# Cached attention decode on one core: each load of keys and values issued as two halves, by SyncE and by ScalarE

## The chip, the cores and the metric

The kernel runs on one core of a Trainium2 chip. The metric is the device time of one execution in microseconds (us), the median of the runs shown; less is better. The profile is of one further execution, and its times are in us from its own start.

## What is computed

One token of a small transformer block: layer norm, attention of 32 heads over a cache of 32768 keys and values of 128 numbers each, a residual, then layer norm and an MLP with the mish activation. All arrays are bfloat16. Cut to what matters:

```python
def _A_ref(x, k_cache, v_cache, wq, wo):          # x [1,1,512], caches [1,32,32768,128]
    q = (x @ wq).reshape(1, 1, 32, 128).transpose(0, 2, 1, 3)
    scores = jnp.einsum("bhqd,bhkd->bhqk", q, k_cache) * (128 ** -0.5)
    p = softmax(scores)
    o = jnp.einsum("bhqk,bhkd->bhqd", p, v_cache)
    return o.transpose(0, 2, 1, 3).reshape(1, 1, 4096) @ wo

h = x + _A_ref(layernorm(x), ...)
h2 = h + mish_mlp(layernorm(h), w1, b1, w2)       # 512 -> 1376 -> 512
```

The two caches hold 32 x 2 x 8.39 MB = 537 MB; all the weights together are 11 MB. Every byte of them is read once.

## The kernel before

**Tiles.** A head's keys are one load of 8.39 MB: partition p takes the 256 consecutive keys 256p to 256p+255, a run of 64 KB, as 256 tiles of 128 x 128 (r-th tile: the r-th key of every partition). Values are laid out the same way. SBUF has a buffer `ring` of six slots of 32 KB a partition: slots 0 and 1 are the home of the keys (`khome`), 2 and 3 that of the values, 4 holds wq (later w1 and w2), and in slot 5 lies `kcopy`, room for the keys' last 112 tiles. So there is one home for keys and one for values, and each serves all heads in turn.

**A head** (function `one`, a loop over heads on TensorE and VectorE). TensorE transposes the keys in 32 groups of 8 tiles (L510), VectorE copies each group from PSUM to `ering` (L513), TensorE multiplies it with the query (L481). `soft_max`, `soft_a`, `soft_b` find the maximum over all scores and, with the next head's query (L539, L543), take a few microseconds; ScalarE's exp (L556) writes the weights `pbuf`; `pv` (L524) multiplies them with the values, 256 small matmuls; `oev` (L531) writes the head's output. To free the keys' home early, ScalarE copies their last 112 tiles to `kcopy` as soon as they have landed (L571, `kc`). Groups 0 to 17 are read from the home, 18 to 31 from the copy.

**Who frees what** (`freed_by`). The next head's keys may be loaded when the 18th group has been transposed (`kfree`) and the copy has been made (`kc`). The next head's values may be loaded when the last matmul of `pv` has read the old ones (`free`). wo follows when the keys' home is free at the end, w1 and w2 when the last query has been made (`qm32`).

**The order of loads.** SyncE issues all loads in one list (`order`): wq, then per head keys and values, then wo, w1, w2. It waits for what frees the target, then issues (L364, in `start`). Heads 0, 30 and 31 are `PARTED`: their keys come in two loads, the first 144 tiles to the home and the last 112 straight into `kcopy`, so ScalarE makes no copy there; head 31's first part is cut once more, and its values come in two halves, the second with a semaphore of its own (`s_half`). ScalarE issues two small loads at the start, x (L407) and b1 (L408), ahead of its table load (L410).

**Waits for data.** Slot 0's semaphore `ready[0]` counts the keys' loads, 16 for each; TensorE waits for 16(h+1) ahead of group 0 and ScalarE ahead of its copy. `ready[2]` counts the values' the same way. `ready[1]` and `s_half` are raised by GpSimd for the heads in which they aren't used.

**Loops.** `rounds` writes a head's work as a hardware loop for the engines in `LOOPED`, the waits as multiples of the loop counter; `apart` leaves some heads outside of it. ScalarE has head 0 ahead of its loop and heads 30 and 31 behind it. SyncE and GpSimd have straight-line programs.

Of the kernel before, what the change touches and what calls it, by code (L numbers as in the profile page):

```python
# [11 lines left out]
AXX = mybir.AxisListType.X  # L12

PE, ACT, DVE, POOL, SP = "pe", "act", "dve", "pool", "sp"
LOOPED = {PE: mybir.EngineType.PE, DVE: mybir.EngineType.DVE, ACT: mybir.EngineType.Activation}


def _name(key):
# [162 lines left out]
def build_kernel(nc, A_x, A_k_cache, A_v_cache, A_wq, A_wo, B_w1, B_b1, B_w2, out):  # L181
    D = A_x.shape[-1]
    Dh = 128
    HD = A_wq.shape[1]
    H = HD // Dh
# [10 lines left out]
    SLOT = TPS * Dh  # L196
    HALVES = Sk // (128 * TPS)
    SCOLS = HALVES * TPS
    GT = 8
# [5 lines left out]
    KT = 2 * TPS - CT  # L205
    CG = KT // GT
    LG = CG // 2
# [79 lines left out]
    ready = [sem(f"ready{i}") for i in range(NS)]  # L287
# [21 lines left out]
    def slot_of(what):  # L309
        return HOMES[what[0]]  # L310

    def ready_wait(what):
        return (ready[slot_of(what)], 16 * (what[1] + 1 if what[0] in "kv" else 1))

    def free_name(what):
        return "free" + "_".join(map(str, what))
# [10 lines left out]
        return []  # L327

    def flat_of(what):
        if what[0] == "v":  # L330
            return ring[:, HALVES:2 * HALVES, :].rearrange("p s x -> p (s x)")
        return ring[:, slot_of(what), :]
# [22 lines left out]
    def program(S):  # L355
# [7 lines left out]
        def start(dst, src, s):  # L363
            S.dma(SP, lambda: sp.dma_start(dst, src).then_inc(s, 16))  # L364

        for what in order:
            slot = slot_of(what)
            S.wait(SP, freed_by(what))
            flat = flat_of(what)
            if what[0] == "wq":  # L370
                start(flat, A_wq.rearrange("(p k) n -> p (k n)", k=KC), ready[slot])
            elif what[0] == "wo":
                j0, j1 = WO_J[what[1]:what[1] + 2]
                start(wo_f[:, j0 * D:j1 * D], A_wo.rearrange("(p j) n -> p (j n)", j=32)[:, j0 * D:j1 * D], s_wo[what[1]])
            elif what[0] == "w1":
                k0, k1 = W1_K[what[1]:what[1] + 2]
                start(w1_v[:, k0:k1, :], B_w1[k0 * 128:k1 * 128, :].rearrange("(k p) n -> p k n", p=128), s_w1[what[1]])
            elif what[0] == "w2":
                j0, j1 = W2_J[what[1]:what[1] + 2]
                if j1 <= FJ:  # L380
                    start(w2_v[:, j0:j1, :], B_w2[j0 * 128:j1 * 128, :].rearrange("(p j) n -> p j n", j=j1 - j0), s_w2[what[1]])
                else:
                    start(w2_v[0:FLAST, FJ, :], B_w2[FJ * 128:F, :], s_w2[what[1]])
            else:
                cache = A_k_cache if what[0] == "k" else A_v_cache
                rows = cache[0, what[1], :, :].rearrange("(p r) d -> p (r d)", r=SCOLS)
                if what[0] == "k" and what[1] not in PARTED:
                    start(khome, rows, ready[slot])
                elif what[0] == "k" and what[2] == 0:
                    cut = [0, KT * Dh] if what[1] < H - 1 else [0, LG * GT * Dh, KT * Dh]  # L390
                    for n, (c0, c1) in enumerate(zip(cut, cut[1:])):
                        start(khome[:, c0:c1], rows[:, c0:c1], ready[n])
                elif what[0] == "k":
                    start(kcopy, rows[:, KT * Dh:], sems["kc"])
                elif what == ("v", H - 1):
                    start(flat[:, 0:SLOT], rows[:, 0:SLOT], ready[slot])
                    start(flat[:, SLOT:], rows[:, SLOT:], s_half)
                else:
# [9 lines left out]
        S.dma(ACT, lambda: a.dma_start(b1r[:, 0:F], B_b1.rearrange("(o n) -> o n", o=1)).then_inc(s_b1, 16))  # L408
        if S.emit and S.only == ACT:
            a.preload_act_table_set("natural_log_exp_and_others")  # L410
# [155 lines left out]
        def one(n):  # L566
            h = n - 1
            if h in PARTED:
                S.lands("kc", f"kc{h}")
            else:  # L570
                S.step(ACT, lambda: a.copy(kcopy, khome[:, KT * Dh:]), name=f"kc{h}", kind="kc", by=16,  # L571
                       waits=[(ready[0], 16 * (h + 1)), f"kend{h - 1}"])
# [118 lines left out]
```

## Time and profile before

| | before |
|---|---|
| median of 3 runs (lowest to highest) | 1274.91 us (1274.8 to 1275.26) |
| profiled execution, span | 1272.9 us |
| bytes read from HBM | 548.08 MB |
| mean granted TensorE clock | 0.769 |

The span runs from the first to the last instruction of the profiled execution; the median stands 2.0 us above it. On the page, section 5 lists groups of instructions: line, engine, operation, output and inputs, count, then busy time and mean duration, then the idle time ahead of them and who ended it. The groups that carry the work of a head:

```profile
L510 PE MATMUL tps<-identb,ring 128*128 128x128 bf16 x8192 | 664.4, 231 | 176.0 <-DMA ring<-in_A_k_cache_dram 176.0
L513 DVE COPY ering<-tps 128x1024 bf16<-128x1024 bf16 x1024 | 668.3, 692 | 226.3 <-PE tps L510 225.4
L571 ACT COPY ring<-ring 128x14336 bf16<-128x14336 bf16 x29 | 352.0, 12139 | 388.7 <-DMA ring<-in_A_k_cache_dram 388.7
L481 PE MATMUL sps<-qcur,ering 128*128 128x1 bf16 x8192 | 343.1, 164 | 10.9 <-DVE ering L513 6.6
L524 PE MATMUL ops<-pbuf,ring 128*128 128x1 bf16 x8192 | 228.5, 165 | 32.3 <-ACT pbuf L556 27.2
L556 ACT ACTIVATE pbuf<-sps,nbias 128x256 bf16<-128x256 f32 x32 | 15.2, 474 | 478.0 <-DVE nbias L553 478.0
```

TensorE's matmuls overlap, so their busy times are larger than the time they fill. In the rows of a timeline the first two numbers are the start and the length of a merged stretch; SPq and ACTq are the instruction queues of SyncE and ScalarE, where DMA issues show.

### The profile page before, as it was taken

How to read it: one execution, taken by the hardware profiler on the slowest of the kernel's cores; microseconds unless marked ns; L12 is line 12 of the kernel's file. 1: busy time of each engine (PE TensorE's matmuls, PEld its weight loads, DVE VectorE, ACT ScalarE, POOL GpSimd, SP SyncE). 2: the span in 40 equal slices, each digit the busy share in tenths (PEclk: the TensorE clock that was granted, in tenths of full speed). 3: DMA queues.
4: the chain of work that ended last, by engine and by line, in shares of the span. 5: the costliest groups of instructions: out<-in, count | busy, mean ns of one | idle time of the engine just before them, and what ended most of it. 6: DMA issues, size and time to landing. Idle time of an engine off the chain costs nothing.

```text
span 1272.9 us, 53513 instructions
## 1 busy us (share of the span) xinstructions
PE 1018.4 (80%) x25146; PEld 993.6 (78%) x25146; DVE 715.2 (56%) x1248; ACT 372.6 (29%) x99; POOL 3.2 (0%) x69
## 2 busy tenths in 40 slices
PE   2777779887779787788877797877897777888996
PEld 2677779787779777788877797877787777888996
DVE  2464446664456654466644566544566444666662
ACT  0033313333213333123332133331233331333000
POOL 0000000000000000000000000000000000000000
PEclk9777778876778877688767788776888677887785
DMA  9999999999999999999999999999999999999998
GB/s 408 439 427 430 435 435 432 441 430 430 432 437 428 445 430 428 432 437 430 432 441 430 430 435 435 428 445 430 428 432 439 428 435 437 432 430 423 446 421 360
DMA packets 11791, 548.24 MB, mean 431 GB/s; under 512 B 1314, under 2 KB 1411, under 8 KB 2564
## 3 DMA queue, kind: packets, MB, share of 16 engines
q1 hardware_dynamic: 11776, 548.08, 99.7%
q8 instruction: 8, 0.13, 0.0%
q14 instruction: 3, 0.02, 0.0%
q10 hardware_dynamic: 4, 0.00, 0.0%
HBM read 548.08 MB, written 0.00 MB: 431 GB/s over the span
## 4 chain that ended last, share of the span: by engine, by line
DMA 63%; PE 35%; ACT 1%; DVE 0%; issue 0%; SPq 0%; ACTq 0%; DVEq 0%
DMA ring<-in_A_k_cache_dram 61%; PE tps L510 27%; PE sps L481 7%; DMA ring<-in_B_w_dram 2%; PE ops L524 1%; ACT ring L571 1%; DVE ering L513 0%; PE tps L641 0%; SPq L364 0%; PE hlp L551 0%; DVE pmax L536 0%; PE hlp L561 0%; ACT pbuf L556 0%; PE hlp L546 0%; DVE gmax L548 0%
## 5 line engine op out<-in xcount | busy, mean ns | idle before, releaser
L510 PE MATMUL tps<-identb,ring 128*128 128x128 bf16 x8192 | 664.4, 231 | 176.0 <-DMA ring<-in_A_k_cache_dram 176.0
L513 DVE COPY ering<-tps 128x1024 bf16<-128x1024 bf16 x1024 | 668.3, 692 | 226.3 <-PE tps L510 225.4
L510 PEld LDWEIGHTS tps<-identb,ring 128*128 128x128 bf16 x8192 | 519.8, 104 | 178.5 <-DMA ring<-in_A_k_cache_dram 178.5
L571 ACT COPY ring<-ring 128x14336 bf16<-128x14336 bf16 x29 | 352.0, 12139 | 388.7 <-DMA ring<-in_A_k_cache_dram 388.7
L481 PE MATMUL sps<-qcur,ering 128*128 128x1 bf16 x8192 | 343.1, 164 | 10.9 <-DVE ering L513 6.6
L481 PEld LDWEIGHTS sps<-qcur,ering 128*128 128x128 bf16 x8192 | 307.8, 97 | 14.0 <-DVE ering L513 9.4
L524 PEld LDWEIGHTS ops<-pbuf,ring 128*128 128x128 bf16 x8192 | 229.7, 105 | 35.1 <-ACT pbuf L556 29.9
L524 PE MATMUL ops<-pbuf,ring 128*128 128x1 bf16 x8192 | 228.5, 165 | 32.3 <-ACT pbuf L556 27.2
L556 ACT ACTIVATE pbuf<-sps,nbias 128x256 bf16<-128x256 f32 x32 | 15.2, 474 | 478.0 <-DVE nbias L553 478.0
L531 DVE TENSOR_TENSOR oT<-ops,rtotc 128x1 f32 x32 | 5.2, 161 | 167.1 <-PE ops L524 167.1
L563 DVE RECIPROCAL rtotc<-hlp 128x1 f32<-128x1 f32 x32 | 5.4, 168 | 95.9 <-PE hlp L561 95.9
L551 PEld LDWEIGHTS hlp<-gmax,onesmat 1*128 1x128 f32 x64 | 11.9, 230 | 21.6 <-DVE gmax L548 21.6
L551 PE MATMUL hlp<-gmax,onesmat 1*128 1x1 f32 x64 | 14.6, 295 | 11.8 <-DVE gmax L548 11.8
L536 DVE TENSOR_REDUCE pmax<-sps 128x1 f32<-128x256 f32 x32 | 13.6, 424 | 14.3 <-PE sps L481 14.3
L561 PE MATMUL hlp<-esum,onesmat 128*128 128x1 f32 x64 | 18.1, 352 | 0.0
L539 PE MATMUL yps<-xnT,ring 128*128 128x1 bf16 x128 | 16.3, 172 | 0.0
L546 PE MATMUL hlp<-ident,pmax 128*1 128x128 f32 x64 | 12.5, 276 | 4.6 <-DVE pmax L536 3.1
L561 PEld LDWEIGHTS hlp<-esum,onesmat 128*128 128x128 f32 x64 | 16.1, 312 | 0.0
L548 DVE TENSOR_REDUCE gmax<-hlp 1x1 f32<-1x128 f32 x32 | 8.9, 278 | 11.9 <-PE hlp L546 11.9
L553 DVE TENSOR_SCALAR nbias<-hlp 128x1 f32<-128x1 f32 x32 | 5.1, 158 | 17.6 <-PE hlp L551 17.6
L539 PEld LDWEIGHTS yps<-xnT,ring 128*128 x128 | 12.3, 96 | 2.0
L546 PEld LDWEIGHTS hlp<-ident,pmax 128*1 128x1 f32 x64 | 2.7, 80 | 7.3 <-DVE pmax L536 7.3
(64 smaller groups left out, 45.4 us busy)
## 6 DMA issues: line engine op xcount, KB each, us to landing
ring<-in_A_k_cache_dram SPq DMA_DIRECT2D x3, 3584.0 KB, 22.4
ring<-in_A_k_cache_dram SPq DMA_DIRECT2D x2, 4608.0 KB, 20.2
ring<-in_A_v_cache_dram SPq DMA_DIRECT2D x2, 4096.0 KB, 25.7
ring<-in_A_k_cache_dram SPq DMA_DIRECT2D x2, 2304.0 KB, 20.0
ring<-in_A_wq_dram SPq DMA_DIRECT2D x1, 4096.0 KB, 12.5
ring<-in_A_wo_dram SPq DMA_DIRECT2D x1, 1792.0 KB, 22.9
ring<-in_A_wo_dram SPq DMA_DIRECT2D x1, 1280.0 KB, 25.7
ring<-in_B_w_dram SPq DMA_DIRECT2D x2, 512.0 KB, 19.9
```

The costliest lines, as they stand in the source:

```text
L481: S.step(PE, lambda r=r: t_.matmul(S_ps[:, col0 + r:col0 + r + 1], ering[:, bg % NE, r, :], qcur[:, :], start=True, stop=True), name=(name ...
L510: S.step(PE, lambda r=r: t_.matmul(tb[:, r * 128:(r + 1) * 128], kt[:, t0 + r, :], identb[:, :], is_transpose=True, start=True, stop=True) ...
L513: S.step(DVE, lambda: v.tensor_copy(ering[:, bg % NE, :, :].rearrange("p r d -> p (r d)"), tb[:, :]), name=f"ev{bg}", waits=[f"trb{bg}", f ...
L524: S.step(PE, lambda r=r, last=last: t_.matmul(o_ps[:, 0:1], vt[:, r, :], pbuf[:, r:r + 1], start=(r == 0), stop=last), name=([free_name((" ...
L536: S.step(DVE, lambda: v.tensor_reduce(pmax[:, :], S_ps[:, 0:SCOLS], AXX, ALU.max), name=f"pmax{h}", waits=[f"qkh{h}"], kind="pmax")
L539: S.step(PE, lambda kc=kc: t_.matmul(Q_REG, wq_v[:, kc, bass.ds((S.index(h + 1) % H) * Dh, Dh)], xnT[:, 0, kc:kc + 1], start=(kc == 0), st ...
L546: S.step(PE, lambda: t_.matmul(A_REG, pmax[:, :], ident[:, :], start=True, stop=True), name=f"A{h}", waits=[f"pmax{h}", "ident"], kind="A")
L548: S.step(DVE, lambda: v.tensor_reduce(gmax[:, :], A_REG, AXX, ALU.max), name=f"gmax{h}", waits=[f"A{h}"], kind="gmax")
L551: S.step(PE, lambda: t_.matmul(B_REG, onesm[0:1, :], gmax[:, :], start=True, stop=True), name=f"B{h}", waits=[f"gmax{h}", "consts0"], kind ...
L556: S.step(ACT, lambda: a.activation(pbuf[:, :], S_ps[:, 0:SCOLS], ACTF.Exp, bias=nb[:, :], scale=SC, accum_out=esum[:, :]), name=f"exp{h}", ...
L561: S.step(PE, lambda: t_.matmul(C_REG, onesm[:, :], esum[:, :], start=True, stop=True), name=f"C{h}", waits=[f"exp{h}"], kind="C")
L571: S.step(ACT, lambda: a.copy(kcopy, khome[:, KT * Dh:]), name=f"kc{h}", kind="kc", by=16, waits=[(ready[0], 16 * (h + 1)), f"kend{h - 1}"])
```

## The change

Each load of keys and values to the two homes becomes two: SyncE issues the first half of every partition's run, ScalarE the second half on its own DMA queue. Both raise the same semaphore, so the waits count 32 for a head in place of 16. For the parted heads it is the first part of the keys that is halved (for head 31 the first 72 of its tiles), and for head 31's values the first of its two halves; the rest of those loads, and all loads of weights, stay with SyncE as they were. ScalarE issues head 0's halves after its table load, the next head's keys behind its copy of the current ones, and the next head's values behind the exp, when `pv` has ended. ScalarE leaves `LOOPED`, so its program is written out for all heads.

```diff
-LOOPED = {PE: mybir.EngineType.PE, DVE: mybir.EngineType.DVE, ACT: mybir.EngineType.Activation}
+LOOPED = {PE: mybir.EngineType.PE, DVE: mybir.EngineType.DVE}
...
     def ready_wait(what):
-        return (ready[slot_of(what)], 16 * (what[1] + 1 if what[0] in "kv" else 1))
+        return (ready[slot_of(what)], 32 * (what[1] + 1) if what[0] in "kv" else 16)
...
+        def rows_of(what):
+            cache = A_k_cache if what[0] == "k" else A_v_cache
+            return cache[0, what[1], :, :].rearrange("(p r) d -> p (r d)", r=SCOLS)
+
+        def shared(what):
+            if what[0] == "k" and what[1] in PARTED:
+                return (LG * GT if what[1] == H - 1 else KT) * Dh
+            return SLOT if what == ("v", H - 1) else 2 * SLOT
+
+        def start_one(what):
+            c = shared(what) // 2
+            start(flat_of(what)[:, 0:c], rows_of(what)[:, 0:c], ready[slot_of(what)])
+
+        def start_other(what, waits=()):
+            c = shared(what)
+            dst, src = flat_of(what)[:, c // 2:c], rows_of(what)[:, c // 2:c]
+            S.dma(ACT, lambda: a.dma_start(dst, src).then_inc(ready[slot_of(what)], 16), waits=waits)
...
-                if what[0] == "k" and what[1] not in PARTED:
-                    start(khome, rows, ready[slot])
-                elif what[0] == "k" and what[2] == 0:
-                    cut = [0, KT * Dh] if what[1] < H - 1 else [0, LG * GT * Dh, KT * Dh]
-                    for n, (c0, c1) in enumerate(zip(cut, cut[1:])):
-                        start(khome[:, c0:c1], rows[:, c0:c1], ready[n])
-                elif what[0] == "k":
+                rows = rows_of(what)
+                if what[0] == "k" and what[1] in PARTED and what[2]:
                     start(kcopy, rows[:, KT * Dh:], sems["kc"])
+                    continue
+                start_one(what)
+                if what[0] == "k" and what[1] == H - 1:
+                    start(khome[:, LG * GT * Dh:KT * Dh], rows[:, LG * GT * Dh:KT * Dh], ready[1])
                 elif what == ("v", H - 1):
-                    start(flat[:, 0:SLOT], rows[:, 0:SLOT], ready[slot])
                     start(flat[:, SLOT:], rows[:, SLOT:], s_half)
-                else:
-                    start(flat, rows, ready[slot])
...
             a.preload_act_table_set("natural_log_exp_and_others")
+        start_other(("k", 0, 0))
+        start_other(("v", 0))
...
                 S.step(ACT, lambda: a.copy(kcopy, khome[:, KT * Dh:]), name=f"kc{h}", kind="kc", by=16,
-                       waits=[(ready[0], 16 * (h + 1)), f"kend{h - 1}"])
+                       waits=[(ready[0], 32 * (h + 1)), f"kend{h - 1}"])
+            if h < H - 1:
+                start_other(("k", h + 1, 0), freed_by(("k", h + 1, 0)))
...
             pv(h, 64, SCOLS)
+            if h < H - 1:
+                start_other(("v", h + 1), freed_by(("v", h + 1)))
             oev(h)
...
-        S.rounds(1, H + 1, one, apart={ACT: (1, 2)})
+        S.rounds(1, H + 1, one, apart={})
```

More of the change, by code (lines that the diff above doesn't have):

```diff
@@ L329, in flat_of @@
     def flat_of(what):
+        if what[0] == "k":
+            return khome
         if what[0] == "v":
@@ L384, in program @@
             else:
-                cache = A_k_cache if what[0] == "k" else A_v_cache
-                rows = cache[0, what[1], :, :].rearrange("(p r) d -> p (r d)", r=SCOLS)
-                if what[0] == "k" and what[1] not in PARTED:
-                    start(khome, rows, ready[slot])
-                elif what[0] == "k" and what[2] == 0:
-                    cut = [0, KT * Dh] if what[1] < H - 1 else [0, LG * GT * Dh, KT * Dh]
-                    for n, (c0, c1) in enumerate(zip(cut, cut[1:])):
-                        start(khome[:, c0:c1], rows[:, c0:c1], ready[n])
-                elif what[0] == "k":
+                rows = rows_of(what)
+                if what[0] == "k" and what[1] in PARTED and what[2]:
                     start(kcopy, rows[:, KT * Dh:], sems["kc"])
+                    continue
+                start_one(what)
+                if what[0] == "k" and what[1] == H - 1:
+                    start(khome[:, LG * GT * Dh:KT * Dh], rows[:, LG * GT * Dh:KT * Dh], ready[1])
                 elif what == ("v", H - 1):
-                    start(flat[:, 0:SLOT], rows[:, 0:SLOT], ready[slot])
                     start(flat[:, SLOT:], rows[:, SLOT:], s_half)
-                else:
-                    start(flat, rows, ready[slot])
         S.dma(SP, lambda: sp.dma_start(spare[0:128:32, :], A_x[0, 0, :].rearrange("(c m) -> c m", c=KC)).then_inc(s_x, 16),
```

## The prediction

> **What bounds the kernel now.** I read the page's head, its DMA queues and its chain first.
>
> ```profile
> span 1272.9 us, 53513 instructions
> ...
> PE 1018.4 (80%) x25146; PEld 993.6 (78%) x25146; DVE 715.2 (56%) x1248; ACT 372.6 (29%) x99; POOL 3.2 (0%) x69
> ...
> q1 hardware_dynamic: 11776, 548.08, 99.7%
> ...
> HBM read 548.08 MB, written 0.00 MB: 431 GB/s over the span
> ...
> DMA 63%; PE 35%; ACT 1%; DVE 0%; issue 0%; SPq 0%; ACTq 0%; DVEq 0%
> ```
>
> One queue, q1, fed by SyncE, keeps the 16 DMA engines occupied for 99.7% of the span. The chain names TensorE for a third, so the second question is whether TensorE's time is a bound or only runs beside the transfers. The timeline of ScalarE answers it: the copy of K's last 112 tiles (L571) starts as soon as a head's keys have landed, once a head, 29 times. Its first two and last rows:
>
> ```profile
> 72.73 12.14 ACT L571 COPY ring<-ring 128x14336 bf16<-128x14336 bf16 x1 [18.45 <-DMA ring<-in_A_k_cache_dram]
> ...
> 111.42 12.14 ACT L571 COPY ring<-ring 128x14336 bf16<-128x14336 bf16 x1 [12.75 <-DMA ring<-in_A_k_cache_dram]
> ...
> 1156.36 12.14 ACT L571 COPY ring<-ring 128x14336 bf16<-128x14336 bf16 x1 [12.97 <-DMA ring<-in_A_k_cache_dram]
> ```
>
> (1156.36 - 72.73) / 28 = 38.70 us a head. A head is two loads of 128 x 64 KB, 16.78 MB, so 433.5 GB/s, or 19.35 us a load. That is the steady state's whole time. TensorE waits in it:
>
> ```profile
> PE tps L510 <- DMA ring<-in_A_k_cache_dram: 176.0, 30, 10.6
> ```
>
> Some 5.9 us of every head TensorE has nothing to transpose. The queue, in turn, never runs empty in the steady state. SyncE's issues, and the start of TensorE's work on the keys of one head:
>
> ```profile
> 65.35 0.33 SPq L364 DMA_DIRECT2D ring<-in_A_v_cache_dram  x1
> 86.07 0.33 SPq L364 DMA_DIRECT2D ring<-in_A_k_cache_dram  x1
> 106.17 0.33 SPq L364 DMA_DIRECT2D ring<-in_A_v_cache_dram  x1
> ...
> 415.00 0.33 SPq L364 DMA_DIRECT2D ring<-in_A_v_cache_dram  x1
> 434.31 0.33 SPq L364 DMA_DIRECT2D ring<-in_A_k_cache_dram  x1
> ```
>
> ```profile
> 420.92 3.59 PE L510 MATMUL tps<-identb,ring 128*128 128x128 bf16 x32 [5.95 <-DMA ring<-in_A_k_cache_dram]
> ```
>
> The values issued at 415.00 go in behind keys that land at 420.92: 5.9 us of work still lies ahead of them. At 106.17 it was least, 5.1 us (those keys landed just before their copy at 111.42, at 111.3). The keys issued at 434.31 have the values before them in flight until 420.9 + 19.35 = 440.2, 5.9 us. So an issue may be up to 5.1 us later at no cost, less what passes from an issue to the first bytes. The end of the chain shows that the tail is again a transfer:
>
> ```profile
> 1246.10 20.57 DMA ring<-in_B_w_dram
> ```
>
> The last of w1 lands at 1266.67, and 6.2 us of work follow it. Whatever shortens or lengthens the stream of 548 MB moves the end by as much; nothing else does.
>
> **The change part by part.**
>
> *Two issues in place of one.* SyncE keeps its issue (0.33 us); ScalarE gets 64 of its own, two a head, at the 0.21 to 0.52 us of its rows below. It is busy 29% of the span, so this hides under its idle time.
>
> ```profile
> 53.72 0.47 ACT L556 ACTIVATE pbuf<-sps,nbias 128x256 bf16<-128x256 f32 x1 [43.02 <-DVE nbias L553]
> ...
> 446.34 0.47 ACT L556 ACTIVATE pbuf<-sps,nbias 128x256 bf16<-128x256 f32 x1 [13.18 <-DVE nbias L553]
> ```
>
> Which work is queued behind? A head's order on ScalarE is copy (L571), wait for kfree and kc, issue K's second half, exp, wait for the end of PV, issue V's second half, copy. The keys' issue waits for what the old one waited for, and ScalarE has made that copy itself; the exp comes only 12 us after that (446.34 against 434.31). The values' issue waits for PV's end; the next copy stands behind it, but its keys land 5.1 to 5.9 us after. So no copy, exp or half-load comes later: 0. If that cover were gone, each microsecond would be one of the stream.
>
> *The loop of ScalarE unrolled.* Code that runs once must be fetched once. TensorE's first pass of its loop shows the price, the stalls put down to "issue":
>
> ```profile
> PE sps L481 <- issue: 4.3, 3, 2.2
> ...
> PE ops L524 <- issue: 3.3, 2, 3.1
> ```
>
> The first and the last of these five:
>
> ```profile
> 34.30 0.25 PE L481 MATMUL sps<-qcur,ering 128*128 128x1 bf16 x4 [0.33 <-issue]
> ...
> 63.23 2.09 PE L524 MATMUL ops<-pbuf,ring 128*128 128x1 bf16 x73 [3.10 <-issue]
> ```
>
> They all lie in head 0, 7.6 us together. TensorE's body is some 1570 instructions (25146 matmuls and as many weight loads over 32 heads), ScalarE's new code a few hundred (the page's 99, 64 issues, the waits), so one or two such stalls. Each can delay one issue by up to 3.1 us, against a lead of 5.1 us less 1.8 us of latency (from the rows at the start), 3.3 us. That just fits: 0, at most about 1 us if one falls in the wrong place.
>
> *Rows of 32 KB in place of 64 KB.* The bytes stay; rows and completion marks double. The tail has loads in parts, on one queue: the keys of heads 30 and 31, the values of 31. First the issue of the last values' two halves, then the second half's microseconds from issue to landing, then from the chain the keys of head 29:
>
> ```profile
> 1222.48 0.80 SPq L364 DMA_DIRECT2D ring<-in_A_v_cache_dram  x2
> ```
>
> ```profile
> ring<-in_A_v_cache_dram SPq DMA_DIRECT2D x1, 4096.0 KB, 30.4
> ```
>
> ```profile
> 1130.79 25.42 DMA ring<-in_A_k_cache_dram
> ```
>
> Head 29's keys land at 1130.79 + 25.42 = 1156.21. The second half of the last values, issued about 1222.9, lands at 1253.3. Between lie five loads, the values of heads 29 and 30 whole, 30's keys in two parts, 31's in three, 31's values in two: 97.1 us, against 5 x 19.35 = 96.75. Four extra cuts for 0.35 us: 0.085 us each, and with the rounding of the view 0.06 to 0.11. The change makes 64 cuts more. In one queue that is 5.4 us. But these were cuts in one queue, where a row's beginning can hide behind nothing; with two queues loaded, each engine has the other's row to move meanwhile. The trace has no stretch with two loaded queues, so the term lies between 5.4 and a gain: the window 200:400 moved
>
> ```profile
> DMA packets 1495, 86.90 MB, mean 435 GB/s; under 512 B 169, under 2 KB 169, under 8 KB 169
> ```
>
> 435 GB/s over 200 us (partly whole packets counted at its edges); a stream that held it would need 548.08 / 435 = 1259.9 us in place of 548.08 / 433.5 = 1264.3, a gain of 4.4. I take 0: the engines are full already, and the cost of a cut looks like one that overlap hides. The Trainium skill, page "DMA: Bandwidth & Descriptors", section "Rules for kernel authors", speaks against the change here: spreading transfers over several issuing engines brings no bandwidth, since all share the same 16 engines, and only saves issue time. By it the term is 0 as well, without the gain.
>
> *The start.* This is the one place where an order changes. Rows of the first 73 us:
>
> ```profile
> 0.74 0.52 ACTq L407 DMA_DIRECT2D ering<-in_A_x_dram  x1
> 0.74 0.40 SPq L364 DMA_DIRECT2D ring<-in_A_wq_dram  x1
> ...
> 1.30 0.21 ACTq L408 DMA_DIRECT2D ering<-in_B_b_dram  x1
> ...
> 1.54 1.28 ACT L410 ACT_TABLE_LOAD   x1 [1.54 <-PEq L676]
> ...
> 2.50 0.37 PE L426 MATMUL hlp<-identb,ering 1*128 1x1 bf16 x8 [2.50 <-DMA ering<-in_A_x_dram]
> ...
> 8.01 0.51 PE L430 MATMUL hlp<-identb,ering 1*128 1x1 bf16 x11 [5.13 <-DMA ering<-in_B_b_dram]
> ...
> 13.37 0.25 PE L461 MATMUL yps<-xnT,ring 128*128 128x1 bf16 x4 [3.69 <-DMA ring<-in_A_wq_dram]
> ...
> 24.20 3.22 PE L510 MATMUL tps<-identb,ring 128*128 128x128 bf16 x32 [10.58 <-DMA ring<-in_A_k_cache_dram]
> ```
>
> ```profile
> 36.99 35.58 DMA ring<-in_A_k_cache_dram
> ```
>
> x shows an issue's latency: 0.74 to 2.50, 1.8 us. b1, one row on ScalarE's queue, issued at 1.30 behind wq's issue, is in by 8.01, while wq's rows run on to 13.37: the second queue is served between the first one's rows, not after them. (The Trainium skill, same page, section "Queues, rings and completion order", says that an engine takes its loaded queues in turn, packet by packet; this row agrees.) I take equal shares. wq, 4.19 MB at 433.5, is 9.7 us, so the stream starts in effect at 3.5. ScalarE's halves come after its table load, 2.82 against 0.74: 2.1 us later, at 5.6. SyncE has by then moved 0.9 MB of the 6.55 (wq 4096 KB and K's first half 2304 KB); the other 5.65 at half the rate take 26.1, and ScalarE's half of K is in before. Head 0's keys are ready at 31.7 in place of 24.2, 7.5 later (9.6, if ScalarE's issue doesn't stand behind the table load), because values that nobody needs yet travel beside them. The stream itself loses nothing so far. But the loop of buffers does: head 1's values were issued 41.15 us after head 0's keys (24.20 to 65.35), so now at 72.85, and head 1's keys, the last bytes in flight, land at 36.99 + 35.58 = 72.57. The queues run empty: 72.85 + 1.8 - 72.57 = 2.1 us, or 4.2 at the other bound. Against it, TensorE's stalls in those 41 us fetch code through the same engines behind 64 KB rows, and 32 KB rows should make them shorter; a third off the 7.6 leaves nothing of the 2.1. I take 1.0, between 0 and 4.2. Head 0's values themselves, through the stream by 51.9 (20.97 MB) to 53, share it from 46.3 on with head 1's second half of keys (issued at 36.99 + 7.5), so they are in at 57 to 60; the exp ahead of their use moves from 53.72 to 61, so they are in time, just. From head 1 on, the lead of an issue is as before.
>
> *The sum.* Span 1272.9 + 1.0 (start) + 0 (rows) + 0 (code) = 1273.9. The median shown, 1274.91, is 2.0 above the span; so 1275.9, rounded 1276. What a measurement can tell from no change is about 0.2%, 2.5 us: the forecast is no change, its own range 1273 to 1277.5.
>
> **The rivals.**
>
> *A, slower: a cut costs with two queues what it costs with one.* Place: every row boundary on the 16 engines. 64 x 0.085 = 5.4, plus 1.0: 1281.3. It decides from 0.025 us a cut (1.6 with the start's 1.0 makes 2.5). For it: the tail's measured 0.35 us, and engines with no idle time to absorb anything. Against: none of those cuts had a second loaded queue. Chance 0.26.
>
> *B, slower: the start's hole at its full size.* TensorE's stalls don't shrink and ScalarE's issue comes early, 4.2 us, with a code stall of ScalarE beyond its lead, 1: 1280. Chance 0.08.
>
> *C, faster: two queues fill the gaps between rows.* 4.4 gained, 1.0 lost at the start: 1271.5. Against: 99.7% leaves 0.3%, 3.8 us, at best. Chance 0.11. The Trainium skill gives 435 GB/s as the ceiling of the engines' ports (same page, "Specifications"); by that figure the estimate for the stream is 1259.4, so much and no more.
>
> *That the change doesn't do what it says:* if the two queues were served one after the other, the halves would land as the whole did, and the time stays 1275 to 1276; it is part of the forecast.
>
> **How the numbers follow.** Forecast 0.55, A 0.26, B 0.08, C 0.11. Faster 0.10 (nearly all of C), slower 0.33 (A and B, less a little), same 0.57. The range runs from 1272.5 (most of C cut off) to 1282, which takes in B and most of A.
>
> **What would show it.** In the changed profile ScalarE's queue should carry 64 issues and somewhat under half of the bytes. Step by step: the copies at L571's place start 38.70 us apart (A: 38.87, C: 38.57); TensorE's first transposes near 32, not 24; the values of head 1 issued near 71 to 73 and its keys landing near 72.6; a gap in DMA of 0 to 4 us right there and none later; the lead of each later issue near 5 us on both queues. I am wrong if the period moves by more than 0.08 us, if keys land with one half well behind the other, or if the queues run empty in the steady state.

## The result and the profile after

| | before | after |
|---|---|---|
| median of 4 runs (lowest to highest) | 1275.03 us (1274.8 to 1275.26) | 1284.41 us (1282.03 to 1287.83) |
| profiled execution, span | 1272.9 us | 1282.0 us |

The ratio of the times is 1.0076, 95% interval 1.0064 to 1.0088: the changed kernel is slower by 9.4 us. The prediction had 1276 and a range up to 1282, so it was wrong. The runs also lie further apart, 5.8 us against 0.5.

The page of the changed kernel, its head, DMA queues and chain:

```profile
span 1282.0 us, 53523 instructions
...
q1 hardware_dynamic: 11776, 288.43, 52.6%
q10 hardware_dynamic: 9220, 259.66, 47.1%
...
HBM read 548.08 MB, written 0.00 MB: 428 GB/s over the span
...
DMA 64%; PE 34%; ACT 1%; DVE 0%; issue 0%; SPq 0%; ACTq 0%; DVEq 0%
```

The change does what it says: ScalarE's queue (q10) carries 47% of the time. The engines are as full as before, 99.7%, the bytes are the same, and the rate is lower. So time is lost inside of a full stream, or in short holes that a mean over the span hides. The copies of K's last tiles, now L587, mark the landing of each head's keys, as long as ScalarE isn't still held at an issue that stands ahead of the copy. These are the first two, the fifth and the last on ScalarE's timeline:

```profile
72.97 12.14 ACT L587 COPY ring<-ring 128x14336 bf16<-128x14336 bf16 x1 [11.57 <-DMA ring<-in_A_k_cache_dram]
114.20 12.14 ACT L587 COPY ring<-ring 128x14336 bf16<-128x14336 bf16 x1 [15.14 <-DMA ring<-in_A_k_cache_dram]
...
231.42 12.14 ACT L587 COPY ring<-ring 128x14336 bf16<-128x14336 bf16 x1 [12.83 <-DMA ring<-in_A_k_cache_dram]
...
1164.05 12.14 ACT L587 COPY ring<-ring 128x14336 bf16<-128x14336 bf16 x1 [13.18 <-DMA ring<-in_A_k_cache_dram]
```

Before, the fifth stood at 227.53:

```profile
227.53 12.14 ACT L571 COPY ring<-ring 128x14336 bf16<-128x14336 bf16 x1 [12.78 <-DMA ring<-in_A_k_cache_dram]
```

Three stretches, three losses. Up to the fifth copy, 3.9 us are lost, 2.5 of them between the first two, which are 41.23 us apart; the next gaps are 39.39, 38.98 and 38.85 us. From the fifth to the last, 24 heads, the period is (1164.05 - 231.42) / 24 = 38.86 us, against 38.70: 0.16 a head, 3.8 us. From the last copy to the end it is 117.95 us against 116.54: 1.4 us.

### The profile page after: what moved, and what is told of

Its sections match the earlier page's. It is cut to its first block, busy times and chain, and to the rows that moved or that the text cites. A ratio compares the mean times of both kernels' runs of the same rounds, so it can differ in the third digit from the quotient of the medians.

```text
span 1282.0 us, 53523 instructions
## 1 busy us (share of the span) xinstructions
PE 1024.4 (80%) x25146; PEld 999.9 (78%) x25146; DVE 716.4 (56%) x1248; ACT 372.6 (29%) x99; POOL 3.2 (0%) x69
## 4 chain that ended last, share of the span: by engine, by line
DMA 64%; PE 34%; ACT 1%; DVE 0%; issue 0%; SPq 0%; ACTq 0%; DVEq 0%
DMA ring<-in_A_k_cache_dram 63%; PE tps L526 26%; PE sps L497 7%; DMA ring<-in_B_w_dram 1%; ACT ring L587 1%; PE ops L540 1%; PE tps L661 0%; DVE ering L529 0%; SPq L366 0%; PE hlp L567 0%; ACT pbuf L572 0%; PE sps L639 0%; ACTq L421 0%; DVE pmax L552 0%; PE hlp L577 0%
## 5 line engine op out<-in xcount | busy, mean ns | idle before, releaser
L526 PE MATMUL tps<-identb,ring 128*128 128x128 bf16 x8192 | 671.2, 233 | 181.1 <-DMA ring<-in_A_k_cache_dram 181.1
L587 ACT COPY ring<-ring 128x14336 bf16<-128x14336 bf16 x29 | 352.0, 12139 | 383.5 <-DMA ring<-in_A_k_cache_dram 383.5
L540 PEld LDWEIGHTS ops<-pbuf,ring 128*128 128x128 bf16 x8192 | 229.5, 105 | 31.5 <-ACT pbuf L572 30.2
L540 PE MATMUL ops<-pbuf,ring 128*128 128x1 bf16 x8192 | 228.1, 165 | 28.8 <-ACT pbuf L572 26.4
## 6 DMA issues: line engine op xcount, KB each, us to landing
ring<-in_A_k_cache_dram SPq DMA_DIRECT2D x29, 4096.0 KB, 24.2
ring<-in_A_k_cache_dram ACTq DMA_DIRECT2D x29, 4096.0 KB, 25.8
```

The costliest lines, as they stand in the source:

```text
L526: S.step(PE, lambda r=r: t_.matmul(tb[:, r * 128:(r + 1) * 128], kt[:, t0 + r, :], identb[:, :], is_transpose=True, start=True, stop=True) ...
L540: S.step(PE, lambda r=r, last=last: t_.matmul(o_ps[:, 0:1], vt[:, r, :], pbuf[:, r:r + 1], start=(r == 0), stop=last), name=([free_name((" ...
```

## The experiments

Theory R: a row of a load costs its DMA engine a fixed time beside its bytes, and the change has twice as many rows. Rival Q: two loaded queues cost something by taking turns. For the start, theory H: the queues are out of step, a load lands late, what it frees is issued late, and the stream runs dry. Each time is compared with the kernel before on the same chip, whose median was 1274.8 to 1275.0 us.

### 1. The cuts without the second queue (cuts_one_queue)

```diff
         def start_one(what):
-            c = shared(what) // 2
-            start(flat_of(what)[:, 0:c], rows_of(what)[:, 0:c], ready[slot_of(what)])
+            c = shared(what)
+            for c0, c1 in ((0, c // 2), (c // 2, c)):
+                start(flat_of(what)[:, c0:c1], rows_of(what)[:, c0:c1], ready[slot_of(what)])
...
         def start_other(what, waits=()):
+            return
```

ScalarE's loop is as before.

> The cuts of the changed kernel without its second queue: the same halves of 32 KB rows, both issued by SyncE one behind the other, ScalarE's loop as before. Theory R (a row costs a fixed time on its engine, whatever the queue): the copies stand 38.86 us apart as in the changed kernel, the start is that of the kernel before (TensorE's first transposes near 24), so about 1275.0 + 31 x 0.16 = 1280. Rival Q (two loaded queues cost something by taking turns, rows cost nothing): 38.70 us apart and 1275.

Measured: 1279.76 us, ratio 1.0038 (1.0025 to 1.0051). The first two copies, the fifth and the last:

```profile
73.20 12.14 ACT L586 COPY ring<-ring 128x14336 bf16<-128x14336 bf16 x1 [19.02 <-DMA ring<-in_A_k_cache_dram]
112.05 12.14 ACT L586 COPY ring<-ring 128x14336 bf16<-128x14336 bf16 x1 [13.24 <-DMA ring<-in_A_k_cache_dram]
...
228.62 12.14 ACT L586 COPY ring<-ring 128x14336 bf16<-128x14336 bf16 x1 [13.39 <-DMA ring<-in_A_k_cache_dram]
...
1161.20 12.14 ACT L586 COPY ring<-ring 128x14336 bf16<-128x14336 bf16 x1 [13.47 <-DMA ring<-in_A_k_cache_dram]
```

(1161.20 - 228.62) / 24 = 38.86: the whole loss of the steady state is there with one queue. The second queue adds 932.63 - 932.58 = 0.05 us over 24 heads, nothing. There is no hole behind the first copy: 38.85 us. Theory R holds and Q falls for the steady state. The Trainium skill, page "DMA: Bandwidth & Descriptors", section "Rules for kernel authors", says that several issuing engines bring no bandwidth; two queues at 38.86 and one at 38.86 agree.

### 2. The cut doubled (quarters_one_queue)

Against run 1:

```diff
-            for c0, c1 in ((0, c // 2), (c // 2, c)):
+            for n in range(4):
+                c0, c1 = n * c // 4, (n + 1) * c // 4
                 start(flat_of(what)[:, c0:c1], rows_of(what)[:, c0:c1], ready[slot_of(what)])
```

The waits count 64 a head.

> The halves on one queue cut once more: every shared load in four issues by SyncE, rows of 16 KB, ScalarE's loop as before. Theory R: a cut costs 0.079 us a load (half of 0.157 us a head), so three cuts 0.47 us a head: 39.17 us between copies, and with head 0 and the tail 1275 + 3 x 4.9 = 1289.7. Rival: if it were the number of loads in flight or their issue and not the rows, SyncE's longer issue is hidden and the period stays near 38.86, about 1280.

Measured: 1289.54 us, ratio 1.0114 (1.0099 to 1.013). The first and the last of its 29 copies:

```profile
73.39 12.14 ACT L587 COPY ring<-ring 128x14336 bf16<-128x14336 bf16 x1 [20.62 <-DMA ring<-in_A_k_cache_dram]
...
1170.08 12.14 ACT L587 COPY ring<-ring 128x14336 bf16<-128x14336 bf16 x1 [13.85 <-DMA ring<-in_A_k_cache_dram]
```

(1170.08 - 73.39) / 28 = 39.17 us. One cut of each load costs 0.16 us a head, three cost 0.47: linear, 0.078 us for each cut of a load, whatever the size of the pieces (32 KB or 16 KB rows). That price is for 8 more rows and one more completion mark on each of the 16 engines. The rows in the DMA traces show the same: between 300 and 1000 us a row of 64 KB (kernel before) takes 2.422 us on average, one of 32 KB (run 1) 1.217 and one of 16 KB (run 2) 0.615, so each further row costs some 0.012 us. Eight of them make 0.10 us a cut, a little more than the 0.078 that the period shows.

### 3. Two queues without new rows (odd_even_partitions)

```diff
-            c = shared(what) // 2
-            start(flat_of(what)[:, 0:c], rows_of(what)[:, 0:c], ready[slot_of(what)])
+            c = shared(what)
+            start(flat_of(what)[0:128:2, 0:c], rows_of(what)[0:128:2, 0:c], ready[slot_of(what)])
...
-            dst, src = flat_of(what)[:, c // 2:c], rows_of(what)[:, c // 2:c]
+            dst, src = flat_of(what)[1:128:2, 0:c], rows_of(what)[1:128:2, 0:c]
```

> The changed kernel, halved by odd and even partitions: SyncE takes 0, 2, 4 and on, ScalarE 1, 3, 5 and on, rows of 64 KB. Theory R with the rate of whole loads kept: 38.70 to 38.74 us between copies, the start's hole as before, 1278 to 1279.5. Rival, if the slow stream of the halves 0 to 63 and 64 to 127 comes of any load over 64 partitions: about 77 us between copies again, 2500.

Measured: 1284.35 us, ratio 1.0077 (1.0062 to 1.0092). Two copies 16 heads apart:

```profile
427.28 12.14 ACT L587 COPY ring<-ring 128x14336 bf16<-128x14336 bf16 x1 [12.97 <-DMA ring<-in_A_k_cache_dram]
...
1046.69 12.14 ACT L587 COPY ring<-ring 128x14336 bf16<-128x14336 bf16 x1 [13.36 <-DMA ring<-in_A_k_cache_dram]
```

619.41 / 16 = 38.71 us. With rows of 64 KB two queues have the old period, though there are twice as many loads and marks: it is the rows. (Of the 24 periods behind the fifth copy two, outside of these 16, are longer, 39.33 and 39.39 us; why isn't known. The mean of all 24 is 38.76.) The total, though, was missed by 5 us: the start's loss is greater here than in the changed kernel. The first copy shows why:

```profile
75.67 12.14 ACT L587 COPY ring<-ring 128x14336 bf16<-128x14336 bf16 x1 [9.44 <-PE ops L540]
```

It waited for PV (L540), not for a DMA. Head 1's keys were in at 72.7 (issued at 47.10, 25.6 to the landing), and its values were issued only at 75.05; the copy stands behind that issue on ScalarE. So the stream was dry: from 70 to 75 us hardly a row began, 7 GB/s. Why the issue comes late is the subject of runs 6 to 10.

### 4. Halves by partitions 0 to 63 and 64 to 127 (partition_halves, partition_halves_one_queue)

```diff
+            start(flat_of(what)[0:64, 0:c], rows_of(what)[0:64, 0:c], ready[slot_of(what)])
...
+            dst, src = flat_of(what)[64:128, 0:c], rows_of(what)[64:128, 0:c]
```

This was the first try at run 3's question.

> The changed kernel, but a load is halved by partitions: SyncE takes partitions 0 to 63, ScalarE 64 to 127, so every row keeps its 64 KB and only the number of loads doubles. Theory R: the copies stand 38.70 to 38.74 us apart (as many rows as before, a few more completion marks); the start still has its hole, about 3 us, so 1278 to 1279. Rival Q: 38.86 us apart and about 1284, as in the changed kernel.

Measured: 2511.79 us, the median of six runs from 2456.9 to 2520.49: twice the time, and no answer to R or Q. Then both halves by SyncE, to see whether it is the two queues:

> Halves by partitions 0 to 63 and 64 to 127 as in the slow run, both issued by SyncE, ScalarE's loop as before. Theory P (a load that goes to only one half of the partitions gets about half of the rate): about 77 us between copies, 2500. Rival (two queues that write different halves at once disturb each other): 38.7 us and 1276.

Measured: 2571.05 us in one run. The second and the last of its copies:

```profile
208.54 12.14 ACT L586 COPY ring<-ring 128x14336 bf16<-128x14336 bf16 x1 [54.97 <-DMA ring<-in_A_k_cache_dram]
...
2379.56 12.14 ACT L586 COPY ring<-ring 128x14336 bf16<-128x14336 bf16 x1 [55.00 <-DMA ring<-in_A_k_cache_dram]
```

(2379.56 - 208.54) / 27 = 80.4 us a head on one queue, so loads that go to partitions 0 to 63 and 64 to 127 move at about half the rate, by whichever queue; odd and even partitions, also 64 to a load, don't. Why was not followed further.

### 5. ScalarE's program written out, alone (scalar_unrolled)

```diff
-LOOPED = {PE: mybir.EngineType.PE, DVE: mybir.EngineType.DVE, ACT: mybir.EngineType.Activation}
+LOOPED = {PE: mybir.EngineType.PE, DVE: mybir.EngineType.DVE}
...
-        S.rounds(1, H + 1, one, apart={ACT: (1, 2)})
+        S.rounds(1, H + 1, one, apart={})
```

> The kernel before with ScalarE's program written out, all loads whole and by SyncE: that part of the change alone. Both theories: 1275.0, the same within 0.2%, periods 38.70. If the fetching of code costs: up to 3 us more, with stalls put down to issue on ScalarE.

Measured: 1274.84 us against 1274.83, ratio 1.0001 (0.9992 to 1.0009). This part of the change costs nothing.

### 6. Head 0 on one queue (head0_one_queue)

In `start_one` SyncE issues both halves for head 0, and `start_other` returns for it.

```diff
+            cuts = (0, c // 2, c) if what[1] in (0,) else (0, c // 2)
...
+            if what[1] in (0,):
+                return
```

> The changed kernel, but head 0's halves are all issued by SyncE in the old order, so nothing travels beside head 0's keys. Theory S (about 3 us of the loss are a hole in the stream where the values of head 1 are issued too late): TensorE starts near 24, the values of head 1 are issued near 65, some 7 us ahead of head 1's keys, whose landing is followed by the next keys' 38.9 us later instead of 41.2; about 1284.4 - 3 = 1281.4. Rival: if the 3 us are another cost of the second queue's first uses, they stay, at 1284.

Measured: 1285.27 us, ratio 1.0076 (1.0063 to 1.0089): no gain, and so the theory in its first form, that head 0's late start makes the loss, fell. The timeline of TensorE shows what took its place:

```profile
63.28 1.84 PE L544 MATMUL ops<-pbuf,ring 128*128 128x1 bf16 x64 [8.47 <-DMA ring<-in_A_v_cache_dram]
```

TensorE waited 8.5 us for head 0's own values. They were SyncE's, behind wq and head 0's keys, while ScalarE's empty queue took up head 1's second half of keys at once. The values landed late, were freed late, and head 1's values were issued at 74.18. Head 1's keys were all in by 72.8 (issued at 38.33, 34.5 to the later landing): as in run 3 the stream was dry, and the first copy was held by ScalarE's own issue:

```profile
74.67 12.14 ACT L591 COPY ring<-ring 128x14336 bf16<-128x14336 bf16 x1 [19.07 <-PE ops L544]
```

The second copy, at 115.70, is again a landing, 42.9 us behind 72.8: 4 us lost. So a queue that is ahead of the other need not delay the keys; it delays whatever the slower one carries.

### 7. Both queues with the same bytes from the start (balanced_start)

wq and head 0's last 112 key tiles are halved between the queues too.

ScalarE's side of the edit (SyncE's loads are shortened to match):

```diff
+        S.dma(ACT, lambda: a.dma_start(ring[:, wq_slot, SLOT // 2:], A_wq.rearrange("(p k) n -> p (k n)", k=KC)[:, SLOT // 2:]).then_inc(ready[wq_slot], 16))
         start_other(("k", 0, 0))
+        S.dma(ACT, lambda: a.dma_start(kcopy[:, CT * Dh // 2:], rows_of(("k", 0, 1))[:, KT * Dh + CT * Dh // 2:]).then_inc(sems["kc"], 16))
         start_other(("v", 0))
```

> The changed kernel, but wq and the last 112 key tiles of head 0 are halved between the two queues as well, so that both carry the same bytes from the first row on. Theory H (the start costs about 3 us because ScalarE's queue runs ahead of SyncE's: what it brings early delays what is needed first, head 1's values are issued late and the queues run dry): TensorE starts on head 0's keys near 24.5, head 1's values are issued near 65, the second copy follows the first by 38.9 us in place of 41.2; time 1284.4 - 3 = 1281.4, and the runs agree better among themselves. Rival: the hole belongs to the second queue's use as such; then the second copy again follows 41 us after the first and the time is 1284.

Measured: 1281.88 us, ratio 1.0054 (1.004 to 1.0068); 2.5 us of the loss are gone, as expected within half a microsecond. But the steps named for it didn't come: TensorE started at 27.2 rather than 24.5, head 1's values were issued at 69.56 rather than 65, and the second copy followed the first by 40.54 us rather than 38.9. Equal bytes, but still not in step, since ScalarE's loads go out about a microsecond later, behind x and b1 (run 8 takes that away).

### 8. In step from the first row (in_step_start)

As run 7, but ScalarE issues its halves as its first instructions, and x and b1 come from GpSimd.

```diff
-        S.dma(ACT, lambda: a.dma_start(xr[:, :], A_x[0, 0, :].rearrange("(o n) -> o n", o=1)).then_inc(s_x, 16))
-        S.dma(ACT, lambda: a.dma_start(b1r[:, 0:F], B_b1.rearrange("(o n) -> o n", o=1)).then_inc(s_b1, 16))
+        S.dma(POOL, lambda: g.dma_start(xr[:, :], A_x[0, 0, :].rearrange("(o n) -> o n", o=1)).then_inc(s_x, 16))
+        S.dma(POOL, lambda: g.dma_start(b1r[:, 0:F], B_b1.rearrange("(o n) -> o n", o=1)).then_inc(s_b1, 16))
...
-        if S.emit and S.only == ACT:
-            a.preload_act_table_set("natural_log_exp_and_others")
         wq_slot = slot_of(("wq", 0))
...
         start_other(("v", 0))
+        if S.emit and S.only == ACT:
+            a.preload_act_table_set("natural_log_exp_and_others")
```

> The kernel with the balanced start, but ScalarE issues its half of wq, keys and values as its first instructions, at the moment when SyncE does, and x and b1 are issued by GpSimd. Theory H: the two queues are in step from the first row, TensorE starts near 24.5 in place of 27.2, head 0's values don't come late, head 1's values are issued near 65, the second copy follows the first by 38.9 us: 1278.3 span like the cuts on one queue, with the tail 1279.8 to 1280.8. Rival: the hole behind head 1 stays 1.5 us or more with the queues in step, then a loaded second queue makes it by itself; 1281.9 as with the balanced start.

Measured: 1280.31 us, ratio 1.0042 (1.0028 to 1.0055), 0.5 us above run 1. The first two copies:

```profile
73.33 12.14 ACT L592 COPY ring<-ring 128x14336 bf16<-128x14336 bf16 x1 [17.76 <-DMA ring<-in_A_k_cache_dram]
112.21 12.14 ACT L592 COPY ring<-ring 128x14336 bf16<-128x14336 bf16 x1 [12.77 <-DMA ring<-in_A_k_cache_dram]
```

38.88 us: the hole is gone with two loaded queues, so it doesn't belong to the second queue as such. TensorE started at 24.55, and head 1's values were issued at 67.01, 6.3 us ahead of head 1's keys. The windows of ten microseconds show the difference; first the changed kernel, then this one (columns: window, its length, busy times of PE, PEld, DVE, ACT and POOL, clock, DMA share, GB/s):

```profile
70.00:80.00 10.00, 7.24 (x111) 7.15 (x109) 4.91 (x8) 7.03 (x1) 0.00 (x0) 0.57 0.96 378
```

```profile
70.00:80.00 10.00, 6.69 (x93) 6.69 (x94) 4.38 (x7) 6.67 (x1) 0.00 (x0) 0.55 1.00 429
```

The DMA share hardly falls, 0.96, while the rate falls by 12%: the engines have rows in hand but move them more slowly there. In the trace the first eleven rows of head 1's values, begun between 71.17 and 71.58, took 1.65 to 2.31 us each, against 1.22 on average later. This is the place that the page's mean of 99.7% hides.

### 9. Joining later (join_at_head2)

SyncE alone loads heads 0 and 1 (in halves), ScalarE joins with head 2's keys: the edit of run 6 with `what[1] < 2`.

> The changed kernel, but heads 0 and 1 are loaded by SyncE alone (still in halves), and ScalarE's queue joins with head 2's keys, where an issue has some 6 us of transfers ahead of it. Theory H (the start's loss comes only of the two queues being out of step while the lead is short): head 1's values are issued near 65, the second copy follows the first by 38.9 to 39.3 us, the later ones 38.86; 1279.8 as with the cuts on one queue, and about 0.9 for the tail, so 1280 to 1281. Rival: a hole of 1 us or more moves to where the second queue joins, 1282 and up.

Measured: 1281.99 us, ratio 1.0058 (1.0044 to 1.0072): the rival. The first four copies:

```profile
72.81 12.14 ACT L591 COPY ring<-ring 128x14336 bf16<-128x14336 bf16 x1 [21.37 <-issue]
113.86 12.14 ACT L591 COPY ring<-ring 128x14336 bf16<-128x14336 bf16 x1 [15.18 <-DMA ring<-in_A_k_cache_dram]
150.82 12.14 ACT L591 COPY ring<-ring 128x14336 bf16<-128x14336 bf16 x1 [11.12 <-DMA ring<-in_A_k_cache_dram]
191.33 12.14 ACT L591 COPY ring<-ring 128x14336 bf16<-128x14336 bf16 x1 [14.41 <-DMA ring<-in_A_k_cache_dram]
```

41.05, 36.96, 40.51 us. Up to the third copy nothing is lost (two periods of 38.86 would give 150.53), but the second set of keys lands 2 us late, because ScalarE's empty queue overtakes and SyncE's half comes after the values. The copy of those keys is late by as much, the next keys are issued late (127.10), and the stream loses 1.6 us one head on. The hole moved to one head after the join.

### 10. In step, with rows of 64 KB (in_step_odd_even)

Run 8 with the halves of run 3: both costs taken away.

> The same in-step start, with loads halved by odd and even partitions, rows of 64 KB: both costs of the change taken away, the two queues and the written-out program kept. Theory R and H together: 38.71 us between copies from the first to the last, no hole, 1275.5 to 1276.5. Rival: a part of the loss belongs to two queues as such and stays, 1278 and up.

Measured: 1281.28 us, ratio 1.0049 (1.0035 to 1.0062), a miss by 5 us. The period is the old one; these copies are 16 heads apart, 619.54 / 16 = 38.72:

```profile
424.50 12.14 ACT L592 COPY ring<-ring 128x14336 bf16<-128x14336 bf16 x1 [13.47 <-DMA ring<-in_A_k_cache_dram]
...
1044.04 12.14 ACT L592 COPY ring<-ring 128x14336 bf16<-128x14336 bf16 x1 [13.02 <-DMA ring<-in_A_k_cache_dram]
```

But the hole is back, 73.41 to 114.63, 41.2 us, and the rate from 70 to 80 us is 303 GB/s:

```profile
70.00:80.00 10.00, 9.18 (x182) 9.09 (x182) 5.10 (x9) 6.59 (x1) 0.00 (x0) 0.59 0.77 303
```

TensorE's timeline ahead of it:

```profile
70.64 2.11 PE L545 MATMUL ops<-pbuf,ring 128*128 128x1 bf16 x74 [5.83 <-issue]
```

A stall of 5.8 us in the middle of head 0's PV; in run 8 the longest was 3.4. It is read as a wait for code: in both traces a packet of 16 KB on the instruction queue, q8, ends 1.5 us ahead of the stall's end (69.11 and 70.64 here, 63.30 and 64.86 in run 8). So head 1's values were issued at 72.78, and the keys were in by 72.9 (issued at 38.15, 34.7 to the later landing; the copy came at 73.41, behind ScalarE's issue). The lead was gone for another reason, with the same end. That rows of 64 KB on two queues make the code wait longer is likely from these two runs, no more.

### 11. Keys by SyncE, values by ScalarE, whole (values_by_scalar)

```diff
+            if what[0] == "v" and what[1] > 0:
+                continue
             S.wait(SP, freed_by(what))
...
             pv(h, 64, SCOLS)
+            if h < H - 1:
+                nxt = ("v", h + 1)
+                src = A_v_cache[0, h + 1, :, :].rearrange("(p r) d -> p (r d)", r=SCOLS)
...
+                    S.dma(ACT, lambda: a.dma_start(flat_of(nxt), src).then_inc(ready[slot_of(nxt)], 16), waits=freed_by(nxt))
```

> The kernel before with two queues but no new rows: SyncE issues the keys whole, ScalarE the values of heads 1 to 31 whole, at the places where the changed kernel issues its halves; head 0 stays with SyncE. Theory R (the fixed time is a row's, the queues cost nothing by taking turns): 38.70 us between copies, about 1275. Rival Q (taking turns costs): more than 38.8 us between copies, 1278 and up.

Measured: 1310.18 us, ratio 1.0272 (1.0258 to 1.0286). This run couldn't tell R from Q, because the order of arrival changed: the values no longer stand behind the keys but share with them. The first copy comes at 77.59 in place of 72.73, the second keys are issued late, and the values that were moved early leave nothing to move. Two windows show it; a row counts in the window in which it begins, and takes 2.4 us, so they are to be read together:

```profile
90.00:92.00 2.00, 2.00 (x55) 2.00 (x53) 2.00 (x5) 0.00 (x0) 0.00 (x0) 1.00 1.33 459
92.00:94.00 2.00, 2.00 (x54) 2.00 (x51) 2.00 (x4) 0.00 (x0) 0.00 (x0) 1.00 0.19 66
```

262 GB/s over four microseconds, in the middle of the stream. The 28 periods run from 35.2 to 45.2 us, with a mean of 39.76. It is the largest loss of the kind that theory H describes; how much of it each head's order of arrival explains was not worked out.

### 12. The tail on one queue (balanced_start_tail)

Run 7, and `start_other` returns for heads 30 and 31, whose halves SyncE issues.

```diff
+            cuts = (0, c // 2, c) if what[1] in (H - 2, H - 1) else (0, c // 2)
...
+            if what[1] in (H - 2, H - 1):
+                return
```

> The kernel with the balanced start, and the loads of heads 30 and 31 all issued by SyncE, as before the change, still in halves. Theory H with the tail's part (about 0.9 us beyond the cuts): 1281.4 - 0.9 = 1280.5 at most, and if both parts of the second queue's cost are removed, the 1279.8 of the cuts on one queue. Rival: no change against the balanced start alone.

Measured: 1280.95 us, ratio 1.005 (1.0036 to 1.0063), 0.9 us below run 7; the two ranges, 1280.7 to 1281.88 and 1281.42 to 1283.45, overlap. From the last copy to the end it is 1278.8 - 1161.95 = 116.85 us against 1280.9 - 1162.68 = 118.2. But run 7's profiled execution was its slowest, and 0.7 us of the difference lie ahead of the last copy, where the two kernels load the same way. Nor does the loss at the tail seem to come in every execution with two queues: run 8's profiled one, its slowest, has 118.4 us there, but its other four have spans of 1278.3 to 1278.5, hardly longer than run 1's 1278.3. One row of the changed kernel's chain shows what is late there:

```profile
1218.95 27.04 DMA ring<-in_A_k_cache_dram
```

The last part of head 31's keys takes 27 us from issue to landing, since ScalarE's half of the last values, issued 11 us later, shares with it; in the kernel before the same load took 22.4. How that becomes a microsecond at the end, and when it does, stays open.

## Why the prediction was wrong

The profiled executions close: 1282.0 - 1272.9 = 9.1 us. Of it 5.4 us are the cuts (1278.3 with the cuts on one queue), 2.8 the hole at the start (231.42 - 228.62), 0.05 the rest of the steady state, 0.85 the tail (117.95 - 117.10). By the medians, 4.9 are the cuts and 4.65 the second queue (its start and tail).

**Where it failed first: "Rows of 32 KB in place of 64 KB", "I take 0".** The term measured 5.4 us. The price itself was right: 0.085 us a cut from four cuts of the tail (0.06 to 0.11 with the rounding), 0.078 measured, and rival A's 38.87 us a head came out as 38.86. What fell is the reason for taking 0, that another loaded queue hides a row's fixed time. It hides none: 38.86 us with two queues and with one. I had the right number and talked it away with a mechanism that no row of the trace showed. A had a chance of 0.26; its time, 1281.3, was too low mostly by what the start and the tail cost more.

**Where a size was off: "The start", 1.0.** Head 0's keys were forecast at 31.7, and TensorE began at 31.59. That is in part luck: the sum put ScalarE's issue behind its table load, at 2.82, and it went out at 1.61, for which the same sum gives about 32.9:

```profile
1.61 0.38 ACTq L384 DMA_DIRECT2D ring<-in_A_k_cache_dram  x1
```

TensorE's code stalls shrank, as the prediction thought they might, from 7.6 to 4.1 us:

```profile
PE sps L497 <- issue: 2.9, 2, 1.7
...
PE ops L540 <- issue: 1.2, 1, 1.2
```

The values of head 1 were issued on both queues at 70.2, 2.7 us ahead of the keys' landing at 72.95:

```profile
70.21 0.33 SPq L366 DMA_DIRECT2D ring<-in_A_v_cache_dram  x1
70.22 0.36 ACTq L384 DMA_DIRECT2D ring<-in_A_v_cache_dram  x1
```

By the prediction's own sum (lead against 1.8 us) no hole should have been left; the loss up to the fifth copy was 2.8 us. The mis-sized term is the 1.8, the time from an issue to the first bytes, which came from x, a load of 1 KB. For these halves the view of issues has the landings (both raise one semaphore, and the view gives its first 16 marks to the first issue, so the second row is the later landing):

```profile
ring<-in_A_v_cache_dram SPq DMA_DIRECT2D x1, 4096.0 KB, 21.9
ring<-in_A_v_cache_dram ACTq DMA_DIRECT2D x1, 4096.0 KB, 24.5
```

The later one is at 70.22 + 24.5 = 94.7. The two halves take 38.86 / 2 = 19.4 us of the stream, so they run in effect from 75.3: 5.1 us behind the issue, not 1.8. Two things are in it. The engines don't end a load together: their marks for the last rows of head 1's keys lie between 70.43 and 72.43, so the issue at 70.21 was only 0.2 us ahead of the first engine that ran dry. And the first rows behind that are slow (run 8). With nothing else in flight the distance is smaller: 2.6 us in run 6, where the values issued at 74.18 were in at 96.2 and so ran in effect from 76.8. As an estimate from these runs, an issue needs about 5 us of other transfers ahead of it. With 5.1 (the kernel before) and 6.3 (run 8) nothing was lost, with 3.4 (run 7) 1.7 us, with 3.6 (run 12, 39.69 us between its first copies) 0.8, with 2.7 here 2.4.

**What was not forecast: the tail,** 0.85 us of the second queue beside its cuts in the profiled execution. Its cause is open.

**What held.** ScalarE's issues delay nothing in the steady state; the written-out program costs nothing (run 5, ratio 1.0001); what the stream loses moves the end by as much; the share that ScalarE's queue takes from what is needed first. That no bandwidth is won held as well: rival C, 435 GB/s, didn't come. (Its 1259.4 us should be 1259.9, as the section on the rows has it; nothing hangs on it.) The condition that the prediction set for its 0 on ScalarE, that the values' issue keeps its lead over the next copy, broke only in runs 3, 6 and 10, where the copy did come late.

No version of this study is faster than the kernel before. The best one with halves on two queues is the in-step start, 1280.31 us, and it is left with the cuts.

## What to carry to other kernels

When the DMA engines are full, count rows: a row costs each engine a fixed time beside its bytes (0.078 us for each cut of a 128-row load, with one queue or two), so a load should keep the longest rows it can have and not be split for the sake of a second queue. Two queues that fill the same buffers have to be kept in step: the one that is ahead takes rate from what is needed next, and where each load is only issued when an earlier one has landed, that lateness empties the stream a head later. A copy is a mark of a landing only while the view names the DMA as what it waited for; in runs 3 and 6 it waited for the engine's own issue. And a price measured in the trace is to be kept in the sum until a row, not an argument, takes it out.

## What the runs showed of the hardware

- Loads over partitions 0 to 63 and 64 to 127 run at about half the rate: 80.4 us a head (209 GB/s) with both halves on one queue, 77.5 us on two, against 38.71 with odd and even partitions. Each row of 64 KB took 4.8 to 5.0 us in place of 2.4. The Trainium skill, page "DMA: Bandwidth & Descriptors", section "Rules for kernel authors", advises against two transfers to disjoint partition halves because they serialize on the same engines. By that alone the two would take as long as the whole, as the odd and even partitions do; the halves 0 to 63 and 64 to 127 took twice as long, and the measurement decides.
- The view of issues has ScalarE's halves landing later than SyncE's in the median, 25.8 against 24.2 us for keys, but that is only the order in which it counts the marks of a shared semaphore. The marks of the two queues show no such difference: head 1's values ended at 94.15 us on both. In run 6, where ScalarE's half of head 1's keys ended at 62.7 and SyncE's at 72.4, the view still has the later landing at ScalarE.
